# Decoding the gated product's weights in pairs of tiles

## The chip, the cores and the metric

The kernel runs on one core of one Trainium2 chip. The metric is the device time of one execution in microseconds (us), the median of several runs. PE is the matmul engine, PEld its weight loads, DVE the vector engine, ACT the scalar engine, POOL the third elementwise engine, and SP the engine whose queue issues all the transfers.

## What is computed

Three stages follow one another. The first is a gated linear recurrence over 768 steps for 4 batches of 8 heads (head size 48); its output is one row of 384 for each of 3072 tokens. The second is a gated product with 1536 hidden columns, the third a product through `h - tanh(h)` with 2048 hidden columns.

```python
# 1: per head, decay a = a_re + i a_im with its size limited to 0.999
new_re = ar * S_re - ai * S_im
new_im = ar * S_im + ai * S_re
S_re, S_im = new_re + k v^T, new_im
y[t] = q[t] @ S_re
# 2:
gate = 1 / (1 + exp(-(x @ w_gate)))
x = (gate * (x @ w_val)) @ w_out
# 3:
h = x @ w_in
out = (h - tanh(h)) @ w_out2
```

## The kernel before

The recurrence is worked in 24 chunks of 128 steps (names with c), two chunks to a block (names with j, 12 blocks of 256 tokens). For each chunk ACT and DVE make angles and magnitudes out of the tile `ri` (lines 454 to 516 on ACT, 461 to 562 on DVE), scale and turn q and k (tiles `qk`, `qs`, `ks`, lines 566 to 578 on POOL and DVE), and PE makes scores, outputs and a new state (lines 617 to 682). Line 600 or 602 copies a chunk's output into `x`, the input of the gated product.

The weights of the gated product are 36 tiles of 128x384 in DRAM: for each of 12 slices f of hidden columns, tiles 0 and 1 (gate and value, both used in line 884 or 888) and tile 2 (the way back, line 930 or 935). They arrive as 64-bit words, two int32 to a weight, and are decoded on the chip by class `Decoder`, one tile to a `tick`: a transfer into a place for raw words (line 286), two ACT instructions in `word_sign` (lines 64 and 66), two DVE instructions in `word_value` (lines 72 and 75). There are six places of 384 words (`ring1`); the transfer of tile s waits until tile s-6 has been through line 75. The decoded tiles (`whole`) serve block 0; behind their last use there, `part` splits each into a high part (ACT, line 314) and a low part (DVE or POOL, line 317), tile `whl`, which all the later blocks use. The six places then hold `whl` of slices 4 to 6.

`moe1` walks block by block and slice by slice. Block 0 goes in two halves (A: chunk 0, Z: chunk 1), 24 short steps, and its last six steps alternate with the first six of block 1. Between those steps stand the instructions of the recurrence for later chunks, and `dec1.ready` calls as many ticks as the next slice needs. The first 12 ticks stand ahead of that, spread evenly over the preparation of chunks 0 and 1. On PE, DVE, ACT and POOL a scheduler then settles the order of instructions, with its own timeline; on SP the order is that of the code, so a transfer that waits holds every later one.

From the second block on nothing is decoded for the gated product. The weights of the third stage have a decoder of their own (`dec2`), whose first DVE instruction starts at 359.1 us.

Of the kernel before, what the change touches and what calls it, by code (L numbers as in the profile page):

```python
# [8 lines left out]
F32 = mybir.dt.float32  # L9
F32R = mybir.dt.float32r  # L10
BF16 = mybir.dt.bfloat16
I32 = mybir.dt.int32
U8 = mybir.dt.uint8
AF = mybir.ActivationFunctionType
ALU = mybir.AluOpType
# [6 lines left out]
NF1, NF2 = FF1 // 128, FF2 // 128  # L22
# [22 lines left out]
F_SLOPE = RS[7] * 1e-6 * 0.5566  # L45

POOLED = ((9, 10), (3, 4, 9, 10), (3, 4, 6, 10), (2, 3, 4, 6, 9, 10, 11), (3, 4, 5), (10,))
TICKS, TICK_FROM, TICK_TO, BEFORE = 12, 0.0, 1.0, 0
LEAD, LEAD_BLOCKS = 0.6, 2.5
SKEW = 6  # L50
EARLY = 6
# [5 lines left out]
def word_sign(nc, raw, sg, direct=False):  # L57

    hi = raw[:, :, 1].bitcast(F32)
    if not direct:
        nc.scalar.activation(sg, hi, AF.Sign)
    nc.scalar.activation(hi, hi, AF.Copy, scale=2.0 ** -112)  # L64
    top = raw.rearrange("p c two -> p (c two)").bitcast(U8).rearrange("p (c eight) -> p c eight", eight=8)[:, :, 3]
    nc.scalar.activation(raw[:, :, 0], top, AF.Identity, scale=1.0 / 32.0, bias=-31.0 / 64.0)  # L66


def word_value(nc, raw, sg, w, direct=False):
    if direct:  # L70
        wi = w.bitcast(I32)
        nc.vector.scalar_tensor_tensor(
            wi, raw[:, :, 1], 3, raw[:, :, 0], ALU.logical_shift_left, ALU.bitwise_or
        )
        nc.vector.scalar_tensor_tensor(  # L75
            wi, raw[:, :, 1], -2 ** 31, wi, ALU.bitwise_and, ALU.bitwise_or
        )
    else:
        nc.vector.scalar_tensor_tensor(
            raw[:, :, 0], raw[:, :, 1], 3, raw[:, :, 0], ALU.logical_shift_left, ALU.bitwise_or  # L80
        )
        nc.gpsimd.tensor_tensor(w, raw[:, :, 0].bitcast(F32), sg, ALU.mult)
# [161 lines left out]
def kernel(ctx: ExitStack, tc: tile.TileContext, ri, qk, vv, w1, w2, out):  # L244
    nc = tc.nc
    w1i = w1.bitcast(I32)
# [5 lines left out]
    wp = fast.enter_context(tc.tile_pool(name="wp", bufs=1))  # L252
# [21 lines left out]
    class Decoder:  # L274
        def __init__(self, src, nf, nparts, ring, depth, low, spill=None):
            self.src, self.nparts, self.n, self.ring, self.depth, self.low = src, nparts, nf * nparts, ring, depth, low
            self.spill = spill
            self.W, self.F, self.raw, self.sg = {}, {}, {}, {}
            self.loaded = self.tick_no = 0

        def load(self, upto):
            while self.loaded < min(upto, self.n):
                s = self.loaded
                self.raw[s], self.sg[s] = self.ring(s)
                src = self.src[s // self.nparts, s % self.nparts]
                nc.sync.dma_start(out=self.raw[s], in_=src.rearrange("p (c two) -> p c two", two=2))
                self.loaded += 1

        def tick(self):
            k = self.tick_no  # L290
            self.tick_no += 1
            if self.spill is not None and 0 <= k - 2 < self.n:
                self.split(k - 2)
            if 0 <= k - 1 < self.n:
                self.value(k - 1)
            self.load(k + 1)
            if k < self.n:
                word_sign(nc, self.raw[k], None, True)
            while self.loaded < self.n and self.loaded - self.depth(self.loaded) <= k - 2 and self.loaded <= k + 4:
                self.load(self.loaded + 1)  # L300

        def value(self, s):
            if self.spill is not None:
                word_value(nc, self.raw[s], None, self.sg[s], True)
                return
            f, p = s // self.nparts, s % self.nparts
            self.F[f, p] = whole_tile(f, p)
            word_value(nc, self.raw[s], None, self.F[f, p], True)

        def part(self, f, p, after):  # L310

            w = self.F.pop((f, p))
            hl = wp.tile([128, 2, 384], F32R, tag=f"w{SLOT[f, p]}", name="whl")
            ins = nc.scalar.copy(hl[:, 0], w)
            tc.add_manual_dep(ins.ins, after.ins.name, mybir.DependencyInfo(
                mybir.DependencyClass.NoSync, mybir.DependencyReason.DATA), reason="weights whole until then")
            self.low[(f * self.nparts + p) % len(self.low)].tensor_tensor(hl[:, 1], w, hl[:, 0].bitcast(F32), ALU.subtract)
            self.W[f, p] = hl

        def split(self, s):  # L320
            w = self.sg.pop(s)
            hl = self.raw[s].rearrange("p c two -> p (c two)").rearrange("p (two c) -> p two c", two=2).bitcast(F32R)
            nc.scalar.copy(hl[:, 0], w)  # L323
            eng = self.low[s % len(self.low)]
            eng.tensor_tensor(hl[:, 1], w, hl[:, 0].bitcast(F32), ALU.subtract)  # L325
            self.W[s // self.nparts, s % self.nparts] = hl
            nc.sync.dma_start(out=self.spill[s], in_=hl.bitcast(F32))

        def ready(self, s):
            while self.tick_no < min(s, self.n) + 1:  # L330
                self.tick()

    def ring0(s):
        return (stg.tile([128, 384, 2], I32, tag="raw", name="raw"),
                stg.tile([128, 384], F32, tag="sg", name="sg"))


    SLOT = {}
# [6 lines left out]
    halves = {}  # L345

    def whole_tile(f, p):
        if (f, p) == (NF1 - 1, 2):
            return stg.tile([128, 384], F32, tag="last", name="wlast", bufs=1)
        k, half = (24 + f, p) if p < 2 else (18 + f // 2, f % 2)  # L350
        if half == 0:
            halves[k] = wp.tile([128, 2, 384], F32, tag=f"w{k}", name="whole2")
        return halves[k][:, half]

    def ring1(s):
        return wp.tile([128, 384, 2], I32, tag=f"w{12 + s % 6}", name="raw"), None

    dec1 = Decoder(w1i, NF1, 3, ring1, lambda s: 6, (nc.vector, nc.gpsimd))


    mask = ap1.tile([128, 128], BF16, name="mask")
# [499 lines left out]
    A, Z, ALL = slice(0, CH), slice(CH, N1), slice(0, N1)  # L861
# [7 lines left out]
    until = [0.0]  # L869
# [74 lines left out]
    def moe1(units, extra):  # L944
        done = [0]

        def run_to(at):
            while done[0] < len(units) and units[done[0]][0] < at:
                units[done[0]][1]()
                done[0] += 1  # L950

        last = len(order) - NF1
        for n, (j, f, cols) in enumerate(order):
            if n == last:
                run_to(until[n])
                open2()
            dec1.ready(min(3 * f + 4, 36) if j == 0 and cols is A else 36 if j > 1 else 0)
            gv(n)
            if n >= 1:
                split(n - 1)  # L960
            run_to((until[n] + until[n + 1]) / 2)
            extra(2 * (n - last) + 1)
            if n >= LAG1:
                outp(n - LAG1)
                jo, fo, co = order[n - LAG1]
                if jo == 0 and co is Z:
                    dec1.part(fo, 2, gated[n - 1])
            if n == last - (NB - 3) * NF1 + LAG1:
                early.close()
                gvp[2] = ph1.enter_context(tc.tile_pool(name="pgv2", bufs=1, space=PSUM))  # L970
            gate(n)
            if j == 0 and cols is Z:
                dec1.part(f, 0, gated[n])
                dec1.part(f, 1, gated[n])
            run_to(until[n + 1])
            extra(2 * (n - last) + 2)
# [10 lines left out]
    with tc.manual_schedule(engines={mybir.EngineType.SP}):  # L987
# [1 line left out]
        load_ri(1)  # L989
        load_qk(0)  # L990
        load_v(0)
        dec1.load(2)
        load_qk(1)
        load_v(1)
        setup()
# [21 lines left out]
        def open2():  # L1017
            flag_sum()
            att.close()
            P2["x0"] = ph2.enter_context(tc.tile_pool(name="m2x", bufs=1, side="right"))  # L1020
            P2["xr"] = ph2.enter_context(tc.tile_pool(name="m2r", bufs=2, side="right"))
            P2["h"] = ph2.enter_context(tc.tile_pool(name="p2h", bufs=3, space=PSUM, side="right"))
            P2["t"] = ph2.enter_context(tc.tile_pool(name="m2t", bufs=2, side="right"))
            P2["g"] = ph2.enter_context(tc.tile_pool(name="m2g", bufs=3, side="right"))
# [4 lines left out]
        def load_w2(upto):  # L1029
            while len(W2) < min(upto, 2 * NF2):  # L1030
                s = len(W2)
                hl = wp.tile([128, 2, 384], F32R, tag=f"w{SLOT[s // 3, s % 3]}", name="whl")
                nc.sync.dma_start(out=hl.bitcast(F32), in_=w2d[s])
                W2[s // 2, s % 2] = hl

# [89 lines left out]
        for n in range(LAG2, total + LAG2):  # L1125
            i, f = divmod(n, NF2)
# [79 lines left out]
```

## Time and profile before

| | us |
|---|---|
| median of 3 runs | 1128.53 (1127.44 to 1130.26) |
| the profiled execution, its own time | 1129.34 |
| its span, first to last instruction | 1127.6 |
| PE busy | 1050.3 |
| DVE busy | 885.4 |
| ACT busy | 829.3 |
| POOL busy | 158.4 |

The span is what the views show; the 1.7 us between it and the execution's own time lie outside of the instructions. The profiled execution is 0.8 us above the median. Over the whole span PE is busy for 93%, but that share is an average over a start, in which PE waits for DVE and ACT, and a long stretch in which it hardly waits at all.

### The profile page before, as it was taken

Reading aid. Unit: us, or ns where it says so; the run is one execution under the profiler, and the core shown is the slowest. Engines: PE = TensorE matmul, PEld = TensorE weight load, DVE = VectorE, ACT = ScalarE, POOL = GpSimd, SP = SyncE. Lnnn points to the kernel's source line nnn. Section 1 sums busy time; section 2 is a strip of 40 time slices with the busy share of each in tenths; the row PEclk is TensorE's granted clock in tenths of the full one; section 3 lists DMA queues with packets and bytes.
Section 4 is the critical chain, followed back from the end, with each engine's and each line's share of the span. In section 5 each row is a group of like instructions: output and inputs, shape, how many; then the busy total and the mean of one; then the engine's idle time right before and its main releaser. Section 6 shows DMA issues by size and latency. Waiting matters only on the chain.

```text
span 1127.6 us, 22170 instructions
## 1 busy us (share of the span) xinstructions
PE 1050.3 (93%) x8782; PEld 982.3 (87%) x8782; DVE 885.4 (79%) x1475; ACT 829.3 (74%) x1828; POOL 158.4 (14%) x126
## 2 busy tenths in 40 slices
PE   0597999999999999998999999999999999999996
PEld 0486899899999999997998989999998989999996
DVE  6899885987778798989998743587878788787875
ACT  8698785887878897977988573566767676676764
POOL 2335431011001212122213200000000000000000
PEclk9998999999999999999999999999999999999999
DMA  6356003122112344453344446700101010010000
GB/s 228 129 196 190 29 18 88 36 71 74 46 59 60 129 141 133 136 181 104 124 157 123 154 150 246 259 1 1 56 1 56 1 56 2 1 57 1 28 1 31
DMA packets 36400, 100.21 MB, mean 89 GB/s; under 512 B 4128, under 2 KB 7200, under 8 KB 36288
## 3 DMA queue, kind: packets, MB, share of 16 engines
q1 hardware_dynamic: 36288, 98.71, 26.7%
q8 instruction: 71, 1.16, 0.4%
q14 instruction: 41, 0.34, 0.1%
HBM read 76.68 MB, written 22.02 MB: 88 GB/s over the span
## 4 chain that ended last, share of the span: by engine, by line
PE 64%; DVE 13%; ACT 13%; DMA 6%; issue 3%; POOL 1%; SPq 0%; DVEq 0%; ACTq 0%; POOLq 0%
PE h L1070 18%; PE o L1096 17%; PE gv L888 14%; PE acc L935 7%; DMA ri<-in_ri_dram 3%; DMA raw<-in_w_dram 2%; PE gv L884 2%; PE xps L751 2%; PE sc L716 1%; ACT raw L64 1%; DVE suf L549 1%; ACT raw L66 1%; PE gps L781 1%; DVE gh L912 1%; DVE sg L75 1%
## 5 line engine op out<-in xcount | busy, mean ns | idle before, releaser
L888 PE MATMUL gv<-x,whl 128*128 128x256 f32 x2376 | 314.6, 286 | 3.2 <-ACT x L602 2.6
L888 PEld LDWEIGHTS gv<-x,whl 128*128 128x128 f32 x2376 | 295.4, 192 | 8.4 <-issue 3.4
L1096 PE MATMUL o<-whl,gh 128*128 128x384 f32 x1152 | 216.6, 337 | 0.6 <-ACT gh L1082 0.6
L1070 PE MATMUL h<-x2h,whl 128*128 128x512 f32 x864 | 216.0, 394 | 0.0
L1096 PEld LDWEIGHTS o<-whl,gh 128*128 128x128 f32 x1152 | 203.6, 188 | 9.3 <-ACT gh L1082 0.9
L1070 PEld LDWEIGHTS h<-x2h,whl 128*128 128x128 f32 x864 | 160.9, 188 | 29.9
L935 PE MATMUL acc<-gh,whl 128*128 128x256 f32 x1188 | 174.3, 290 | 2.5 <-DVE gh L912 2.2
L935 PEld LDWEIGHTS acc<-gh,whl 128*128 128x128 f32 x1188 | 153.1, 192 | 7.2 <-DVE gh L912 3.1
L89 ACT ACTIVATE s<-h 128x512 f32<-128x512 f32 x96 | 57.8, 602 | 114.5 <-PE h L1070 114.4
L1083 DVE TENSOR_TENSOR gh<-g,gh 128x512 fp32r<-128x512 f32 x96 | 66.3, 690 | 43.8 <-ACT gh L1082 43.5
L912 DVE TENSOR_TENSOR gh<-g,gh 128x256 fp32r<-128x256 f32 x132 | 73.9, 561 | 30.3 <-ACT gh L911 29.2
L97 DVE TENSOR_TENSOR th<-h,th 128x512 f32<-128x512 f32 x96 | 66.4, 691 | 31.6 <-ACT th L95 30.7
L896 ACT ACTIVATE th<-gv 128x256 f32<-128x256 f32 (+1 forms) x156 | 56.3, 361 | 38.8 <-PE gv L888 30.4
L903 DVE SCALAR_TENSOR_TENSOR g<-th,gv 128x256 f32<-128x256 f32 x132 | 54.3, 413 | 37.8 <-ACT th L896 36.7
L98 DVE COPY_PREDICATED g<-mk,th 128x512 f32<-128x512 int32 x96 | 72.3, 754 | 1.0
L911 ACT CAST gh<-g 128x256 fp32r<-128x256 f32 x132 | 52.8, 401 | 26.2 <-DVE g L903 25.7
L91 DVE SCALAR_TENSOR_TENSOR g<-g,s 128x512 f32<-128x512 f32 x96 | 65.5, 682 | 3.3 <-ACT g L90 3.3
L1082 ACT CAST gh<-g 128x512 fp32r<-128x512 f32 x96 | 59.2, 617 | 11.3 <-DVE g L98 11.0
L92 DVE TENSOR_TENSOR g<-g,h 128x512 f32<-128x512 f32 x96 | 65.0, 678 | 3.1
L566 POOL TENSOR_TENSOR qk<-qk,suf 112x512 f32<-112x512 f32 x21 | 31.2, 1484 | 253.3 <-DMA qk<-in_qk_dram 102.4
L325 POOL TENSOR_TENSOR raw<-sg,raw 128x384 fp32r<-128x384 f32 x32 | 40.6, 1269 | 166.7 <-ACT raw L323 129.1
L96 ACT ACTIVATE mk<-s 128x512 f32<-128x512 f32 x96 | 60.8, 633 | 0.0
(165 smaller groups left out, 1697.5 us busy)
## 6 DMA issues: line engine op xcount, KB each, us to landing
raw<-in_w_dram SPq DMA_DIRECT2D x68, 384.0 KB, 5.1
ri<-in_ri_dram SPq DMA_DIRECT2D x30, 448.0 KB, 5.3
w2d<-raw SPq DMA_DIRECT2D x32, 384.0 KB, 4.1
whl<-w2d SPq DMA_DIRECT2D x32, 384.0 KB, 5.0
qk<-in_qk_dram SPq DMA_DIRECT2D x24, 448.0 KB, 4.9
v<-in_vv_dram SPq DMA_DIRECT2D x24, 320.0 KB, 3.5
x2d<-x SPq DMA_DIRECT2D x12, 384.0 KB, 2.3
x2r<-x2d SPq DMA_DIRECT2D x12, 384.0 KB, 3.7
```

The lines of the kernel that those rows point to most:

```text
L91: nc.vector.scalar_tensor_tensor(g, g, TC * TB, s, ALU.add, ALU.mult)
L92: nc.vector.tensor_tensor(g, g, ps, ALU.mult)
L96: nc.scalar.activation(mk, s, AF.Relu, bias=-0.0625)
L97: nc.vector.tensor_tensor(th, ps, th, ALU.subtract)
L98: nc.vector.copy_predicated(g, mk.bitcast(I32), th)
L888: nc.tensor.matmul(ps[:, part], w[:, wi, cs], x[:, xi, kt], start=(k == 0), stop=(k == 8))
L912: nc.vector.tensor_tensor(gh[:, 1], g, gh[:, 0].bitcast(F32), ALU.subtract)
L935: nc.tensor.matmul(o, w[:, wi, cs], gh[:, gi], start=(f == 0 and k == 0 and (m == 0 or m == 2 and not half)), stop=(f == NF1 - 1 and k == ...
L1070: nc.tensor.matmul(ps.rearrange("p (z c) -> p z c", z=2), w[:, wi, cs], x[:, xi, :, kt], start=(k == 0), stop=(k == 8))
L1082: nc.scalar.copy(gh[:, 0], g)
L1083: nc.vector.tensor_tensor(gh[:, 1], g, gh[:, 0].bitcast(F32), ALU.subtract)
L1096: nc.tensor.matmul(a[t], gh[:, gi, cs], w[:, wi], start=(f == 0 and k == 0), stop=(f == NF2 - 1 and k == 2), skip_group_check=True)
```

## The change

The class `Twos` takes the place of `Decoder` for the gated product. A step takes two tiles: gate and value of one slice, or tile 2 of two neighbouring slices, in the order g0, o0, g1, g2, o1, g3, and so on, 18 steps (P0 to P17 below). Its transfer, its two ACT instructions and its two DVE instructions each cover both tiles, 768 columns. Only the last step of the kind o has its DVE work in two halves. There are three places for two tiles each (`d0` to `d2`) instead of six for one, in the same amount of memory; the transfer of step s waits until step s-3 has been through line 75, and is issued at most two steps ahead of the ACT work. Six ticks instead of 12 stand in the preparation. The three places hold `whl` of slices 4 to 6 afterwards, as the six did.

```diff
-TICKS, TICK_FROM, TICK_TO, BEFORE = 12, 0.0, 1.0, 0
+TICKS, TICK_FROM, TICK_TO, BEFORE = 6, 0.0, 1.0, 0
...
+    class Twos:
+
+        def __init__(self):
+            self.seq = []
+            for f in range(NF1):
+                self.seq += [("g", f)] + ([("o", f // 2)] if f % 2 == 0 else [])
...
+        def load(self, upto):
+            while self.loaded < min(upto, self.n):
+                s = self.loaded
+                kind, k = self.seq[s]
+                self.raw[s] = wp.tile([128, 2, 384, 2], I32, tag=f"d{s % 3}", name="raw")
+                src = w1i[k, 0:2] if kind == "g" else w1i[2 * k:2 * k + 2, 2]
+                nc.sync.dma_start(out=self.raw[s], in_=src.rearrange("q p (c two) -> p q c two", two=2))
+                self.loaded += 1
+
+        def value(self, s):
+            kind, k = self.seq[s]
+            raw = self.raw.pop(s)
+            if (kind, k) == ("o", NF1 // 2 - 1):
+                for q in range(2):
+                    self.F[2 * k + q, 2] = whole_tile(2 * k + q, 2)
+                    word_value(nc, raw[:, q], None, self.F[2 * k + q, 2], True)
+                return
+            both = wp.tile([128, 2, 384], F32, tag=f"w{24 + k if kind == 'g' else 18 + k}", name="whole2")
+            word_value(nc, raw.rearrange("p q c two -> p (q c) two"), None, both.rearrange("p q c -> p (q c)"), True)
...
+        def tick(self):
+            k = self.tick_no
+            self.tick_no += 1
+            if 0 <= k - 1 < self.n:
+                self.value(k - 1)
+            self.load(k + 1)
+            if k < self.n:
+                word_sign(nc, self.raw[k].rearrange("p q c two -> p (q c) two"), None, True)
+            while self.loaded < self.n and self.loaded - 3 <= k - 2 and self.loaded <= k + 2:
+                self.load(self.loaded + 1)
...
+        def place(self, f, p, dtype):
+            if 4 <= f < 7 and p < 2:
+                if p == 0:
+                    self.six[f] = wp.tile([128, 2, 2, 384], dtype, tag=f"d{f - 4}", name="whl")
+                return self.six[f][:, p]
+            return wp.tile([128, 2, 384], dtype, tag=f"w{SLOT[f, p]}", name="whl")
...
-    def ring1(s):
-        return wp.tile([128, 384, 2], I32, tag=f"w{12 + s % 6}", name="raw"), None
-
-    dec1 = Decoder(w1i, NF1, 3, ring1, lambda s: 6, (nc.vector, nc.gpsimd))
+    dec1 = Twos()
...
-            dec1.ready(min(3 * f + 4, 36) if j == 0 and cols is A else 36 if j > 1 else 0)
+            dec1.ready(dec1.at['g', f] + 2 if j == 0 and cols is A else dec1.n if j > 1 else 0)
...
-        dec1.load(2)
+        dec1.load(1)
...
-                hl = wp.tile([128, 2, 384], F32R, tag=f"w{SLOT[s // 3, s % 3]}", name="whl")
+                hl = dec1.place(s // 3, s % 3, F32R)
```

Lines after 288 move: line 286 is 332 in the changed kernel, and a line between 361 and 956 is 42 higher (line 454 is 496, line 633 is 675).

The scheduler answers with another order in the first part of the program; the last 1490 instructions on DVE and the last 6745 on PE stand as before. Three places follow. The first is on ACT, behind the second table load for the sines (line 510, 552 in the changed kernel), where chunk 1's angles and magnitudes stand beside chunk 0's first transposed keys (`kt`). Before:

```order
L510 ACT_TABLE_LOAD
L633 COPY kt_317<-ktp_318 128x448
L533 ACTIVATE A_266<-ri_127 112x512
L534 ACTIVATE B_267<-ri_127 112x512
L455 ACTIVATE thC_302<-ri_264 112x512
L456 ACTIVATE thB_301<-ri_264 112x512
L538 ACTIVATE C_268<-A_266 112x512
L495 ACTIVATE D_236<-ri_127 112x512
L64 ACTIVATE raw_275<-raw_275 128x384
L66 ACTIVATE raw_275<-raw_275 128x384
```

Of the change, the same place:

```order
L552 ACT_TABLE_LOAD
L575 ACTIVATE A_241<-ri_127 112x512
L576 ACTIVATE B_242<-ri_127 112x512
L580 ACTIVATE C_243<-A_241 112x512
L581 ACTIVATE A_241<-A_241 112x512
L582 ACTIVATE C_243<-C_243 112x512
L537 ACTIVATE D_217<-ri_127 112x512
L538 ACTIVATE D_217<-D_217 112x512
L675 COPY kt_286<-ktp_287 128x448
L497 ACTIVATE thC_278<-ri_239 112x512
```

Seven instructions on chunk 1, which stood behind the copy of `kt`, now stand ahead of it, and no decoding stands near it.

The second place is on DVE, at the same time: the scan over chunk 1's angles (`ri<-keep,ri`). Before:

```order
L75 SCALAR_TENSOR_TENSOR whole_384<-raw,whole_384 128x384
L490 SCALAR_TENSOR_TENSOR ri<-keep,ri 112x512
L72 SCALAR_TENSOR_TENSOR whole_384<-raw 128x384
L75 SCALAR_TENSOR_TENSOR whole_384<-raw,whole_384 128x384
L622 TENSOR_TENSOR pt<-sc_278,mask 128x512
L544 SCALAR_TENSOR_TENSOR B<-A,B 112x512
```

Of the change:

```order
L620 TENSOR_TENSOR qs<-qk,ri 112x4x128
L532 SCALAR_TENSOR_TENSOR ri<-keep,ri 112x512
L586 SCALAR_TENSOR_TENSOR B<-A,B 112x512
L587 SCALAR_TENSOR_TENSOR A<-C,B 112x512
L591 SCALAR_TENSOR_TENSOR suf<-A,sufs 112x511
L542 SCALAR_TENSOR_TENSOR ri<-D,ri 112x512
```

Behind the scan there stood a tile to decode; now chunk 1's magnitudes follow at once.

The third place is on ACT, further on, where the steps P10 to P14 are decoded (raw_632, raw_639, raw_693, raw_739, raw_746, in this order; `th` is a gate of block 0, `whl` the high part of a split tile). Of the change:

```order
L64 ACTIVATE raw_639<-raw_639 128x768
L66 ACTIVATE raw_639<-raw_639 128x768
L938 ACTIVATE th_705<-gv_695 128x128
L938 ACTIVATE th_724<-gv_711 128x128
L374 CAST whl_728<-whole2_269 128x384
L374 CAST whl_731<-whole2_269 128x384
L374 CAST whl_759<-whole2_224 128x384
L64 ACTIVATE raw_693<-raw_693 128x768
L66 ACTIVATE raw_693<-raw_693 128x768
L64 ACTIVATE raw_739<-raw_739 128x768
L66 ACTIVATE raw_739<-raw_739 128x768
L64 ACTIVATE raw_746<-raw_746 128x768
```

Five steps stand there with two gates and three splits between them; before, no more than three tiles in a row were decoded without another instruction of ACT.

## Rows read from the trace of the kernel before

**Rows 1.** Busy microseconds of each engine in stretches; PEclk is the granted clock share.

```profile
20.00:30.00 10.00, 0.00 (x0) 0.00 (x0) 9.79 (x17) 9.95 (x18) 5.29 (x2) 1.00 0.19 58
30.00:40.00 10.00, 6.04 (x52) 5.15 (x52) 5.72 (x11) 5.47 (x12) 0.91 (x1) 1.00 0.66 223
40.00:50.00 10.00, 7.20 (x67) 6.15 (x68) 10.00 (x20) 9.76 (x21) 3.67 (x2) 1.00 0.30 103
110.00:120.00 10.00, 10.00 (x77) 9.24 (x79) 8.42 (x21) 7.65 (x18) 2.34 (x2) 0.69 0.01 3
130.00:140.00 10.00, 8.11 (x73) 7.80 (x72) 8.81 (x14) 9.08 (x20) 7.91 (x6) 1.00 0.22 73
150.00:160.00 10.00, 10.00 (x90) 9.28 (x89) 6.92 (x12) 7.36 (x20) 1.60 (x2) 1.00 0.01 2
250.00:300.00 50.00, 50.00 (x548) 47.91 (x546) 38.37 (x70) 40.14 (x99) 5.69 (x4) 1.00 0.16 51
```

**Rows 2.** The tile raw up to 140 us: instructions (ns min/median/max), waits, landings.

```profile
L64 ACT ACTIVATE raw<-raw x36: 523/557/590, 12.1 to 107.9; 128x384 f32<-128x384 f32 x36
L75 DVE SCALAR_TENSOR_TENSOR whole<-raw,whole x35: 525/550/2158, 13.7 to 114.6; 128x384 int32<-128x384 int32 x35
  ACT raw L66: 7.1, 5
  DMA raw<-in_w_dram: 0.4, 1
DMA to landing us min/median/max: 2.8/5.6/9.4
```

**Rows 3.** Timeline of ACT: start us, us, then the instruction, wait in brackets.

```profile
11.62 0.61 ACT L455 ACTIVATE thC<-ri 112x512 f32<-112x512 f32 x1
12.13 0.52 ACT L64 ACTIVATE raw<-raw 128x384 f32<-128x384 f32 x1
12.56 0.52 ACT L66 ACTIVATE raw<-raw 128x384 int32<-128x384 uint8 x1
...
28.75 1.28 ACT L510 ACT_TABLE_LOAD   x1
33.46 0.53 ACT L633 COPY kt<-ktp 128x448 f32<-128x448 f32 x1 [3.43 <-PE ktp L632]
```

**Rows 4.** Timeline of DVE, early stretch, same columns.

```profile
13.12 0.56 DVE L72 SCALAR_TENSOR_TENSOR whole<-raw 128x384 int32<-128x384 int32 x1 [3.06 <-ACT raw L66]
13.71 0.56 DVE L75 SCALAR_TENSOR_TENSOR whole<-raw,whole 128x384 int32<-128x384 int32 x1
...
32.16 1.02 DVE L72 SCALAR_TENSOR_TENSOR whole<-raw 128x384 int32<-128x384 int32 x2
33.10 0.69 DVE L472 TENSOR_TENSOR ri<-thA,thC 112x512 f32<-112x512 f32 x1
...
34.71 1.22 DVE L490 TENSOR_TENSOR_SCAN ri<-keep,ri 112x512 f32<-112x512 uint8 x1
39.22 0.56 DVE L72 SCALAR_TENSOR_TENSOR whole<-raw 128x384 int32<-128x384 int32 x1 [3.30 <-ACT raw L66]
```

**Rows 5.** SP's queue: a wait in total, then timeline rows of SP, one of ACT.

```profile
SPq L286 <- DVE whole L75: 31.2, 11, 5.8
...
72.23 17.16 SPq L286 DMA_DIRECT2D raw<-in_w_dram  x9
...
90.70 0.43 SPq L412 DMA_DIRECT2D ri<-in_ri_dram  x1
...
97.69 0.63 ACT L454 ACTIVATE thA<-ri 112x512 f32<-112x512 f32 x1 [2.75 <-DMA ri<-in_ri_dram]
```

**Rows 6.** Timeline of PE and DVE around the first products of block 1.

```profile
57.11 2.93 PE L884 MATMUL gv<-x,whole 128*128 128x128 f32 x12 [5.20 <-DVE gh L900]
...
129.35 0.53 DVE L603 TENSOR_TENSOR x<-xps,x 128x384 fp32r<-128x384 f32 x1
...
131.89 2.40 PE L888 MATMUL gv<-x,whl 128*128 128x256 f32 x18
```

More of the change, by code (lines that the diff above doesn't have):

```diff
@@ L291, in tick @@
             self.tick_no += 1
-            if self.spill is not None and 0 <= k - 2 < self.n:
+            if 0 <= k - 2 < self.n:
                 self.split(k - 2)
@@ L302, in value @@
         def value(self, s):
[L303 to L318, printed above, removed]
+            word_value(nc, self.raw[s], None, self.sg[s], True)
         def split(self, s):
@@ L327, in split @@
             nc.sync.dma_start(out=self.spill[s], in_=hl.bitcast(F32))
+    class Twos:
[3 more added lines that the diff above has]
+                self.seq += [("g", f)] + ([("o", f // 2)] if f % 2 == 0 else [])
+            self.n = len(self.seq)
+            self.at = {u: i for i, u in enumerate(self.seq)}
+            self.W, self.F, self.raw, self.six = {}, {}, {}, {}
+            self.low = (nc.vector, nc.gpsimd)
+            self.loaded = self.tick_no = 0
+        def load(self, upto):
[16 more added lines that the diff above has]
+            word_value(nc, raw.rearrange("p q c two -> p (q c) two"), None, both.rearrange("p q c -> p (q c)"), True)
+            for q in range(2):
+                self.F[(k, q) if kind == "g" else (2 * k + q, 2)] = both[:, q]
+        def tick(self):
[8 more added lines that the diff above has]
+                self.load(self.loaded + 1)
         def ready(self, s):
@@ L331, in ready, with part @@
                 self.tick()
+        def place(self, f, p, dtype):
[4 more added lines that the diff above has]
+            return wp.tile([128, 2, 384], dtype, tag=f"w{SLOT[f, p]}", name="whl")
+        def part(self, f, p, after):
+            w = self.F.pop((f, p))
+            hl = self.place(f, p, F32R)
+            ins = nc.scalar.copy(hl[:, 0], w)
+            tc.add_manual_dep(ins.ins, after.ins.name, mybir.DependencyInfo(
+                mybir.DependencyClass.NoSync, mybir.DependencyReason.DATA), reason="weights whole until then")
+            self.low[(3 * f + p) % 2].tensor_tensor(hl[:, 1], w, hl[:, 0].bitcast(F32), ALU.subtract)
+            self.W[f, p] = hl
     def ring0(s):
@@ L349, in whole_tile @@
             return stg.tile([128, 384], F32, tag="last", name="wlast", bufs=1)
[L350 to L353, printed above, removed]
-    def ring1(s):
-        return wp.tile([128, 384, 2], I32, tag=f"w{12 + s % 6}", name="raw"), None
-    dec1 = Decoder(w1i, NF1, 3, ring1, lambda s: 6, (nc.vector, nc.gpsimd))
+        halves[f] = wp.tile([128, 2, 384], F32, tag=f"w{18 + f // 2}", name="whole2")
+        return halves[f][:, 0]
+    dec1 = Twos()
     mask = ap1.tile([128, 128], BF16, name="mask")
```

## The prediction

> **What bounds the kernel now.** I read the stretches first, since the average over the span hides two regimes. From 150 us on PE is busy without a gap, while DVE and ACT have slack (6.92 and 7.36 of 10 us, later 38.37 and 40.14 of 50) [rows 1]. All decoding for the gated product lies before that: 35 of its 36 tiles start between 12.1 us and 114.6 [rows 2]. In that first part PE starves: 0 of 10 us busy from 20 to 30, 6.04 and 7.20 in the next two stretches, while DVE has 9.79 and later 10.00 of 10, and ACT 9.95 and 9.76 [rows 1]. PE's longest gap behind its start, 5.20 us, ends with a gate on DVE [rows 6]. So the time is a fixed PE stretch behind a start that DVE, and up to 30 us ACT, paces. A microsecond saved on DVE there can be one in the end; one saved at 500 us would be none.
>
> Two rows bound how long that holds. From 110 to 120 us PE is already busy for all 10 us, at 0.69 of its clock, and from 130 to 140 for 8.11 [rows 1]. The first full-precision product of block 1 starts at 131.89, 2.5 us behind the low part of its last input (129.35) on DVE [rows 6].
>
> **The change, part by part.**
>
> *DVE, fewer instructions.* Before, 36 tiles take two each, 72 in all. After, 17 steps take two and the split one four: 38. So 34 starts are removed, and the columns stay. Two independent ones of line 72 take 1.02 us together, one alone 0.56, so the second adds 0.46 [rows 4]. What columns cost I take from line 472: 0.69 us for 512 against 0.56 for line 72's 384 [rows 4], so 128 columns are worth some 0.13 and 384 some 0.39. What a start costs beside columns is 0.46 - 0.39 = 0.07 to 0.08: 34 x 0.08 = 2.7 us. Where line 75 follows its own line 72 directly, the starts lie 13.71 - 13.12 = 0.59 apart, so merging two there saves 0.59 - 0.39 = 0.20: with 17 such pairs and 17 of the other kind, 4.8 us. I take 2.7, since most of the rows are interleaved, and keep 4.8 for the range. It lies on the path, since DVE is full from 40 us.
>
> [...]
>
> *ACT, fewer instructions.* 72 become 36. A start every 0.51 us for 512 columns and 0.43 for 384 [rows 3] leaves 0.08 for 128 columns, so 768 take 0.43 + 3 x 0.08 = 0.67, and 36 mergers save 36 x 0.19 = 6.8 us of ACT. That counts only where DVE waits for ACT. Those waits on decoded words sum to 7.1 us in five cases [rows 2]; 3.06 of them is the first, at 13.12, which hides behind the start of the angles and stays. 3.30 is that of the next paragraph. I put the rest (0.7) at nothing, and the ACT saving itself at nothing: DVE covers it. If DVE were no longer full, up to 6.8 would show.
>
> *The order at 30 to 39 us.* ACT stands idle for 3.43 us ahead of the copy of `kt` (33.46) [rows 3]. Behind the copy stand chunk 1's magnitudes and one tile to decode; DVE, through with its scan at 34.71 + 1.22 = 35.93, waits for that tile until 39.22, 3.30 us [rows 4]. In the changed order seven ACT instructions of 512 columns (7 x 0.51 = 3.6 us) stand ahead of the copy and fill ACT's gap, and DVE has chunk 1's magnitudes ready behind the scan. So the 3.30 goes. What is late next is the angle of chunk 2 (lines 461 and 462 on DVE), which needs the transfer of `ri` and six ACT instructions behind the copy; I leave 0.8 for it, some one and a half of them. Gain 2.5, bounds 0 (another wait of that size) and 3.3.
>
> *Transfers.* As many bytes in 18 instead of 36. Before, a transfer takes 5.6 us to its landing (2.8 to 9.4), and ACT waited for one just once, 0.4 us [rows 2]. After, the first half of a pair waits for the second. SP waits 31.2 us in 11 cases for line 75 to free a place, and the nine transfers from 72.23 on hold the queue for 17.16 us, with the loads of the recurrence behind them; `ri` came so late that ACT waited 2.75 [rows 5]. The changed queue has five transfers there instead of nine, the last of which waits for the same decoded tiles (24), so `ri` comes about as before. I charge 0.8, twice the one wait; bounds 0 and 11 (the second rival).
>
> *Splits, whl and the third stage.* Number and shapes of lines 314 and 317 stay; the tiles in the new places are freed by the same products of slices 4 to 6 as before. Nothing.
>
> **Sum.** -2.7 - 2.5 + 0.8 = -4.4 us. The profiled execution took 1129.34 with a span of 1127.6; it would be 1124.9, and the median, 0.8 lower, 1128.53 - 4.4 = 1124.1.
>
> **Rivals.**
>
> *PE swallows it: no change.* From 110 us on PE has 10.00 of 10, so what DVE does sooner behind that is hidden, and ahead of the first line 888 stand the same 165 products of block 0 as before. For it: PE at 0.69 of its clock from 110 to 120. Against it: the 1.9 us gap from 130 to 140, and that a DVE ahead of time closes the gaps before 110 as well. If only the gain up to 57 us is lost again to a later input of block 1 (129.35), some 1 us is left: 1127.5. It decides if line 603 for chunk 3 ends less than 3 us earlier.
>
> *Three places are too few: slower.* In the third place of the order, P13 needs P10's place and P14 needs P11's. From the end of P11's ACT work to the start of P14's, ACT has two gates, three splits and two steps. Two gates are some 0.4, three splits 3 x 0.43 (their width is line 64's), two steps 4 x 0.67: 4.4 us. In that time P11 must go through DVE (2 x (0.46 + 0.39) = 1.7) and P14's words must land (5.6 as before, 11.2 if twice the bytes take twice the time, 8.4 between). That is 7.3 to 12.9, so ACT waits 2.9 to 8.5, with gates and the angles of chunk 4 queued behind it, and PE and DVE wait for those. With the middle, 5.7, for each of the two rounds of three places from P12 on, 11.4 - 5.2 = +6.2: 1134.7. It decides from 8.6 us of ACT's waits for raw words on (5.2 gained plus 3.4). Against it: the scheduler may have put the rows so late that ACT is never early, and DVE's backlog, not ACT, paces this stretch.
>
> [...]
>
> *The scheduler's new order costs more than it gives, or gives more.* Each way I see some microseconds that no row prices; they widen the range.
>
> **Chances.** A measurement here tells 0.3% (3.4 us) from no change. The forecast 0.46 with its own range of 1119 to 1126; PE swallows it 0.31; the places 0.23. So faster 0.46, same 0.31, slower 0.23. The low end is 4.8 for DVE, 3.3 for the gap and 1.4 of ACT's saving: -9.5, 1119. The high end, 1133, cuts the worst of the second rival.
>
> **What would show it.** Right: 38 instructions of lines 72 and 75 near 0.95 us and 36 of lines 64 and 66 near 0.8; no DVE wait of 3 us near 35; ACT's waits for raw words under 2 us; line 603 for chunk 3 and the first line 888 some 3 to 4 us earlier; PE's rows from 170 us on the same, shifted. Wrong: ACT or SP waiting long for places from 70 to 115 us, or PE's gaps before 110 merely moved.

## The result: slower, by 0.6%

The changed kernel took 1134.92 us (median of 8, 1132.22 to 1138.69), the kernel before in the same runs 1128.61 (median of 8): a ratio of 1.0061, 95% interval 1.0044 to 1.0079. The prediction was 1124.1 with a high end of 1133. The profiled execution took 1133.6, with a span of 1131.6 and the same mean clock, 0.986.

First the stretches of the kernel before, which were not shown, then the same and two more of the changed kernel (columns as in [rows 1]):

```profile
20.00:60.00 40.00, 18.05 (x141) 15.91 (x142) 35.51 (x60) 30.12 (x59) 14.01 (x6) 0.93 0.39 128
60.00:100.00 40.00, 35.10 (x464) 31.88 (x463) 38.37 (x67) 36.18 (x80) 18.70 (x11) 0.94 0.59 199
```

```profile
20.00:60.00 40.00, 20.62 (x165) 18.35 (x166) 39.62 (x55) 31.82 (x54) 11.60 (x7) 1.00 0.44 153
60.00:100.00 40.00, 32.29 (x333) 29.56 (x332) 33.20 (x47) 33.30 (x62) 13.71 (x10) 0.88 0.55 180
...
90.00:100.00 10.00, 4.82 (x29) 4.61 (x28) 8.25 (x10) 7.69 (x15) 4.66 (x3) 0.70 0.95 313
...
130.00:140.00 10.00, 8.77 (x86) 8.33 (x87) 8.08 (x11) 9.46 (x22) 7.14 (x5) 1.00 0.40 125
```

From 20 to 60 us the change does what was forecast: DVE is busy for 39.62 of 40 us instead of 35.51, and PE for 2.57 us more. From 60 to 100 all of it goes: DVE idles for 6.80 us instead of 1.63, and PE does 2.81 less. The instructions that answer to [rows 2], the changed kernel's tile `raw` up to 150 us:

```profile
L64 ACT ACTIVATE raw<-raw x18: 859/914/956, 12.7 to 106.8; 128x768 f32<-128x768 f32 x18
L75 DVE SCALAR_TENSOR_TENSOR whole<-raw,whole x18: 941/950/3262, 15.3 to 117.2; 128x768 int32<-128x768 int32 x17, 128x384 int32<-128x384 int32 x1
  ACT raw L66: 11.1, 7
  DMA raw<-in_w_dram: 2.7, 3
  DVE whole L75: 2.3, 1
DMA to landing us min/median/max: 4.1/7.4/12.4
```

Merged instructions have the forecast length (0.95 us on DVE). But ACT now waits 5.0 us in four cases for raw words (2.7 and 2.3) instead of 0.4, and DVE 11.1 for ACT instead of 7.1. One such wait can be followed from end to end. Timeline rows of the changed kernel, of DVE, ACT (two), DVE (two) and PE:

```profile
86.37 1.37 DVE L75 SCALAR_TENSOR_TENSOR whole<-raw,whole 128x768 int32<-128x768 int32 x1
...
93.48 0.90 ACT L64 ACTIVATE raw<-raw 128x768 f32<-128x768 f32 x1 [2.31 <-DVE whole L75]
...
95.03 0.44 ACT L938 ACTIVATE th<-gv 128x128 f32<-128x128 f32 x2
...
95.18 0.96 DVE L72 SCALAR_TENSOR_TENSOR whole<-raw 128x768 int32<-128x768 int32 x1 [1.72 <-ACT raw L66]
96.06 0.48 DVE L942 SCALAR_TENSOR_TENSOR gh<-th,gv 128x128 f32<-128x128 f32 x2
...
96.39 2.93 PE L926 MATMUL gv<-x,whole 128*128 128x128 f32 x12 [5.18 <-DVE gh L942]
```

The transfers of the same tile that were issued from 86 to 89 us:

```profile
L332 SPq DMA_DIRECT2D raw<-in_w_dram x1: 368/368/368, 87.8 to 87.8; - x1
DMA to landing us min/median/max: 5.6/5.6/5.6
```

Line 75 frees a place at 86.37 + 1.37 = 87.74. SP, whose queue stood at that load, issues it at 87.8, it lands 5.6 us later at 93.4, and ACT starts at 93.48. (The row names line 75 as the releaser, since another one ended at the same moment; the landing fits as well, and that instruction waits for the transfer.) Behind the two ACT instructions stand `th`, the gates' first half, on ACT (95.03), and line 72 on DVE (95.18); behind both stand the gates (line 942, which was 900), and PE, which waits for those, has been idle for 5.18 us. Where it stood idle, from 90 to 100, the granted clock was 0.70 of full speed: 1.00 in each microsecond up to 94, 0.53 in the next and 0.50 from 95 on.

The start of block 1, against [rows 6], on DVE and PE:

```profile
134.58 0.54 DVE L645 TENSOR_TENSOR x<-xps,x 128x384 fp32r<-128x384 f32 x1
...
135.55 2.39 PE L930 MATMUL gv<-x,whl 128*128 128x256 f32 x18
```

Line 645 (before: 603) comes 5.2 us later, the first full-precision product 3.7. That is one part of the loss. Another stands in the last microseconds. Instructions of SP's closing line, of before and then of the changed kernel (whole, and in two windows), and the changed kernel's wait there:

```profile
L1143 SPq EVENT_SEMAPHORE  x8: 17/17/17, 1125.7 to 1126.3; - x8
```

```profile
L1185 SPq EVENT_SEMAPHORE  x8: 17/17/17, 1127.8 to 1130.2; - x8
...
L1185 SPq EVENT_SEMAPHORE  x2: 17/17/17, 1127.8 to 1127.9; - x2
L1185 SPq EVENT_SEMAPHORE  x6: 17/17/17, 1129.8 to 1130.2; - x6
```

```profile
SPq L1185 <- SPq L1185: 4.7, 2, 2.8
```

Before, SP goes through its eight closing waits in 0.6 us; after, it takes 2.4, with 1.9 us between the second and the third. In that gap the transfers of that execution show one single packet, and it is of the queue that carries instructions (window 1127.9 to 1129.8; queue, packets, MB, share):

```profile
q14 instruction: 1, 0.01, 1.4%
```

### The profile page after: what moved, and what is told of

Same layout as the page of the kernel before. It is cut to its first block, busy times and chain, and to the rows that moved or that the text cites. A ratio compares the mean times of both kernels' runs of the same rounds, so it can differ in the third digit from the quotient of the medians.

```text
span 1131.6 us, 22057 instructions
## 1 busy us (share of the span) xinstructions
PE 1053.8 (93%) x8782; PEld 983.9 (87%) x8782; DVE 880.8 (78%) x1441; ACT 826.2 (73%) x1792; POOL 155.1 (14%) x126
## 4 chain that ended last, share of the span: by engine, by line
PE 49%; ACT 20%; DVE 17%; DMA 9%; issue 3%; SPq 0%; DVEq 0%; ACTq 0%
PE h L1112 18%; PE o L1138 17%; DMA ri<-in_ri_dram 7%; PE gv L930 7%; PE acc L977 4%; DMA raw<-in_w_dram 2%; DVE suf L591 1%; ACT raw L64 1%; ACT raw L66 1%; DVE B L604 1%; ACT L552 1%; ACT gh L953 1%; DVE gh L954 1%; ACT th L938 1%; ACT thC L497 1%
## 5 line engine op out<-in xcount | busy, mean ns | idle before, releaser
L954 DVE TENSOR_TENSOR gh<-g,gh 128x256 fp32r<-128x256 f32 x132 | 70.0, 531 | 30.5 <-ACT gh L953 29.5
```

Of the source, the lines that this page charges most:

```text
L954: nc.vector.tensor_tensor(gh[:, 1], g, gh[:, 0].bitcast(F32), ALU.subtract)
```

## Experiments

Each was timed beside the kernel before. Between the measurements the median of the kernel before moved from 1127.4 to 1129.2, so kernels are compared by their ratio to it; 0.001 is 1.13 us. Each interval is some 2 us wide to either side, so a difference between two rows of the table is uncertain by some 3 us, and a smaller one is not shown.

| run | median us | ratio | 95% interval |
|---|---|---|---|
| the change | 1134.92 | 1.0061 | 1.0044 to 1.0079 |
| e1: four places | 1132.96 | 1.0041 | 1.0023 to 1.0059 |
| e2: pairs, 384-column instructions | 1136.12 | 1.0076 | 1.0051 to 1.0102 |
| e3: pairs, single transfers | 1134.62 | 1.0057 | 1.0035 to 1.0080 |
| e4: before, sequence of the change | 1130.69 | 1.0019 | 1.0000 to 1.0037 |
| e5: SP longer by 18 | 1132.06 | 1.0028 | 1.0011 to 1.0046 |
| e6: five places | 1129.92 | 0.9995 | 0.9975 to 1.0015 |
| e7: out tiles later | 1130.50 | 1.0016 | 0.9998 to 1.0033 |
| e8: before, 11 steps early | 1132.26 | 1.0029 | 1.0005 to 1.0053 |
| e9: e5, e6 and e7 together | 1129.96 | 1.0017 | 0.9997 to 1.0036 |
| e10: e9, 384-column instructions | 1133.68 | 1.0050 | 1.0031 to 1.0070 |
| e11: e9, single transfers | 1130.40 | 1.0026 | 1.0007 to 1.0044 |
| e12: e9 with six places | 1127.67 | 0.9998 | 0.9979 to 1.0017 |
| e13: e5 and e6 together | 1127.79 | 0.9991 | 0.9969 to 1.0013 |
| e14: before, 13 steps early | 1130.90 | 1.0012 | 0.9993 to 1.0032 |
| e15: e13, 7 steps early | 1130.97 | 1.0018 | 1.0001 to 1.0036 |
| e16: e13 with six places | 1126.82 | 0.9983 | 0.9966 to 1.0001 |
| e17: e16, 384-column instructions | 1135.94 | 1.0074 | 1.0048 to 1.0100 |
| e18: SP longer by 4 | 1132.10 | 1.0036 | 1.0017 to 1.0055 |

**Places, instructions, transfers, sequence, one at a time (e1 to e4).**

```diff
e1
-self.raw[s] = wp.tile([128, 2, 384, 2], I32, tag=f"d{s % 3}", name="raw")
+self.raw[s] = wp.tile([128, 2, 384, 2], I32, tag=f"d{s % 4}", name="raw")
...
-while self.loaded < self.n and self.loaded - 3 <= k - 2 and self.loaded <= k + 2:
+while self.loaded < self.n and self.loaded - 4 <= k - 2 and self.loaded <= k + 3:
...
-if 4 <= f < 7 and p < 2:
+if 3 <= f < 7 and p < 2:
e2 (word_value alike)
-word_sign(nc, self.raw[k].rearrange("p q c two -> p (q c) two"), None, True)
+for q in range(2):
+    word_sign(nc, self.raw[k][:, q], None, True)
e3
-nc.sync.dma_start(out=self.raw[s], in_=src.rearrange("q p (c two) -> p q c two", two=2))
+for q in range(2):
+    src = w1i[k, q] if kind == "g" else w1i[2 * k + q, 2]
+    nc.sync.dma_start(out=self.raw[s][:, q], in_=src.rearrange("p (c two) -> p c two", two=2))
e4 (on the kernel before, in Decoder)
...
+self.seq += [(f, 0), (f, 1)] + ([(f, 2), (f + 1, 2)] if f % 2 == 0 else [])
...
```

> The changed kernel with four places for raw pairs instead of three (the fourth lies where slice 3's split halves go later, so no memory is added); transfers, 768-column instructions and the first products' place in PE's order stay as in the changed kernel. Theory A (three places are too few: the raw words come late from 80 us on): ACT's 2.7 us of waits for raw words and its 2.3 us wait for line 75 go below 1 us together, SP's 30.6 us of waits for line 75 fall by a third or more, and the time comes back by 3 to 5 us, to 1130 to 1132. Theory B (the scheduler's new order ahead of 60 us, chunk 1's scores in front of block 0's first products): the waits on raw words may go, but the time stays at 1133 to 1137. Theory C (the 768-column instructions themselves, stretched and coarse on DVE): 1133 to 1137 too.

> The changed kernel with its transfers and its three places of two tiles each, but every step decodes its two halves in instructions of 384 columns, so the starts of instructions come back (72 and 72 instead of 38 and 36). Chunk 1's scores stand ahead of the first products in PE's order, as in the changed kernel. Theory C (the 768-column instructions cost it): back to 1128 to 1130. Theories A and B: no gain, 1135 to 1139, the changed kernel's 1134.9 plus up to 2.7 us for the DVE starts that the prediction priced.

> The changed kernel, 768-column instructions and three places of two tiles, but each place is filled by two transfers of 384 KB instead of one of 768 KB. The order in which PE's instructions are written out comes back to that of the kernel before: block 0's first three products stand ahead of chunk 1's scores. Theory B (the order, which the pair transfers bring about): first products at 46 to 48 us again, and the time falls to 1124 to 1129. Theory A (three places): ACT still waits for raw words from 80 us on, and the time stays above 1131. Theory C (768-column instructions): it stays at 1133 to 1137.

> The kernel before, with single tiles, six places and 384-column instructions, but its tiles are loaded and decoded in the sequence of the changed kernel (both gate tiles of a slice, then the out tiles of two slices together). PE's written order of the first products is that of the kernel before. If the sequence of tiles alone cost the time: 1133 to 1136. If, as theories A, B and C all have it, something else did: 1127 to 1130.

The fourth place gives 2 us, less than theory A put on it and within the noise; ACT still waits 3.4 us for words. e2 refutes theory C: with 384 columns the kernel is not faster. e3 does not test theory B. It was written to bring the first products back to 46 to 48 us, but on PE they start where the changed kernel has them, behind 16 of chunk 1's scores (ACT's wait for words is 6.8 us). The first products in the changed kernel, in e3 and, from the last group below, in e13 (five places):

```profile
53.03 4.58 PE L926 MATMUL gv<-x,whole 128*128 128x128 f32 x24
```

```profile
53.62 4.90 PE L927 MATMUL gv<-x,whole 128*128 128x128 f32 x24
```

```profile
55.19 5.49 PE L926 MATMUL gv<-x,whole 128*128 128x128 f32 x24
```

e13 speaks against theory B: its first products stand behind the same 16 scores and come later still (46.83 in the kernel before), and it is no slower than the kernel before. e4, in which the sequence of the tiles is changed and no place, transfer or instruction, is 2 us behind the kernel before, at the edge of the noise.

**SP's end (e5, e18) and five places (e6).**

```diff
e5 (e18: 4 in the place of 18)
-nc.sync.dma_start(out=out[r0:r0 + 128, :], in_=ob)
+if 4 * i + t < 18:
+    for h in range(2):
+        nc.sync.dma_start(out=out[r0:r0 + 128, h * 192:(h + 1) * 192], in_=ob[:, h * 192:(h + 1) * 192])
+else:
+    nc.sync.dma_start(out=out[r0:r0 + 128, :], in_=ob)
e6 (as e1 with five)
-if 4 <= f < 7 and p < 2:
+if 2 <= f < 7 and p < 2:
```

> The changed kernel, with 18 of its first 20 output tiles stored in two halves each, all 40 us or more ahead of the end: SP's program is as many instructions long again as that of the kernel before. Nothing else is changed. In the traces so far SP's eight closing semaphore waits lie within 0.6 us in the three kernels with 36 transfers of raw words, and have a gap of 1.95 us between two of them in the three with 18, at the third or the sixth wait, when every transfer has landed. Theory T (the end of SP's program pays 1.9 us for where its code lies): the gap goes and the time falls by 1.5 to 2.2 us, to about 1133. Against it (the gap is a transfer's late signal, or goes with the pair transfers): the eight waits still take 2.4 us and the time stays at 1134 to 1136.

> The changed kernel with four output tiles stored in halves instead of 18, so SP's program is four instructions longer than the changed kernel's and 14 shorter than that of the kernel before. In the changed kernel the gap of 1.95 us lies between the second and the third of SP's closing waits. If it belongs to a place in SP's code, four more instructions move the waits past it: the eight waits lie within 0.6 us, and the time falls to 1132 to 1133.5, unless the gap then falls on the branch ahead of them and the first wait ends 1.9 us later. If it belongs to the number of transfers of raw words (18 against 36): the gap stays at the third wait and the time at 1134 to 1136.

> The changed kernel with five places for raw pairs (the two more lie where the split halves of slices 2 and 3 go later). Theory A (places, so late raw words that ACT waits for): ACT's waits for raw words, 5.0 us with three places and 3.4 with four, fall below 2, and the time falls below the 1133.0 of four places by another 1 to 2 us, to 1131 to 1132, which is 1129 to 1130 but for the 1.9 us at SP's end. If places are not what costs: 1133 to 1136 as with three or four.

Four instructions more on SP are enough. The closing waits of e18, and the wait in them:

```profile
L1189 SPq EVENT_SEMAPHORE  x8: 17/17/17, 1131.2 to 1131.8; - x8
```

```profile
SPq L1189 <- SPq L1189: 3.4, 1, 3.4
```

The gap is gone although the 18 transfers of raw words are still 18, so it goes with the length of SP's program. That it is the place of SP's closing code, as theory T has it, fits but is not shown directly. The two kernels (e5, e18) gain 2.9 and 2.8 us by their medians (3.7 and 2.8 by the ratios); by the rows 1.9 of that is the gap.

Five places bring 5 us by the medians (7.5 by the ratios), and the gap at SP's end is still in that kernel. That is more than was expected. The wait of SP's loads for line 75 up to 150 us (sum, cases, longest), in the changed kernel, in e6 and then in e16 (six places, below):

```profile
SPq L332 <- DVE whole L75: 30.6, 8, 9.6
```

```profile
SPq L332 <- DVE whole L75: 11.7, 2, 7.1
```

```profile
SPq L332 <- DVE whole L75: 6.6, 1, 6.6
```

**What the sequence and the written order are worth (e7, e8, e14, e15).**

```diff
e7
-self.seq += [("g", f)] + ([("o", f // 2)] if f % 2 == 0 else [])
+self.seq += [("g", f)] + ([("o", f // 2)] if f % 2 == 1 else [])
e8 and e14 (on the kernel before; e14: 13), e15 (on e13, from 6 to 7)
-TICKS, TICK_FROM, TICK_TO, BEFORE = 12, 0.0, 1.0, 0
+TICKS, TICK_FROM, TICK_TO, BEFORE = 11, 0.0, 1.0, 0
```

> The changed kernel with its pairs in another sequence: the out tiles of slices f and f+1 are loaded and decoded behind both slices' gate tiles instead of between them. Theory S (the sequence puts the gate tiles of every odd slice a pair later than they are wanted; the kernel before lost 2.4 us by that sequence alone): 1.5 to 3 us back, 1132 to 1133.5. If the 2.4 us were chance: 1134 to 1136.

> The kernel before with 11 instead of 12 of its decoding steps written out among the setup and the rest behind it: the same work, places, transfers and instructions in a slightly different written order (chunk 1's scores behind the fourth of the first products instead of the third). A control for theory R, that any new order moves the time by as much as this change did: then it would be off by 3 us or more either way, below 1125.5 or above 1131.5. If the order alone is worth less: 1126 to 1131.

> The kernel before with 13 instead of 12 decoding steps among the setup; a second control of what a new written order costs. If the kernel before owes some 2 to 3 us to its own written order (11 steps took 3 us more, the other sequence of tiles 2.4): 1130 to 1133 again. If orders scatter to both sides: 1125 to 1129.

> The kernel with five places and the long SP program, with seven of its steps among the setup instead of six: the same work in a third written order (all of chunk 1's scores behind two first products). If written orders alone scatter by some 3 us: 1124 to 1131, off by 1.5 us or more from the same kernel with six. If the order hardly matters once places suffice: within 1.5 us of it.

e7 gains 4.4 us with three places, more than theory S allowed. But with five places the same edit brings nothing (e13 to e9: 0.9991 to 1.0017), so the sequence has no price of its own: it deals a new order. Read the other way, the same rows limit what can be said of places: in the sequence of e7, five places and the longer SP program bring nothing either (e7 to e9: 1.0016 to 1.0017), though ACT's wait for words falls from 3.6 to 1.0 us, and the first full-precision product of block 1 starts at 131.29 with three places and 131.58 with five. The controls show how much the written order, in which the code hands its instructions to the scheduler, moves alone. The kernel before with one decoding step more or less among the setup is 1.4 and 3.3 us slower by the ratios, and e15 is 3 us off from e13. Each is the same work with the same places. Of these only the 3.3 of e8 is clear of noise; at 1132.26 it is past the 1131.5 that was set as the sign for theory R, so written order remains a rival for some 3 us of any difference here.

**The mends together, and the merged instructions' own price (e9 to e13, e16, e17).**

These are sums of the edits above: e9 is e5, e6 and e7; e10 is e9 and e2; e11 is e6, e7 and e3; e12 is e9 with six places; e13 is e5 and e6; e16 is e13 with six places; e17 is e16 and e2.

> The three mends together: the changed kernel with five places, the out tiles behind both slices' gate tiles, and 18 output tiles stored in halves so that SP's program is as long as before. If the causes add (five places 5.0 us, the sequence 2 to 4.4, SP's end 1.9 to 2.9, against 1134.9): 1123 to 1126, which would be the 4.4 us below the kernel before that the prediction counted for fewer starts and the order at 30 to 39 us. If places and sequence mend the same waits: 1127 to 1129, no faster than the kernel before, and the predicted gain was not there.

> The kernel with the three mends, but decoding in instructions of 384 columns instead of 768, so it prices the merged instructions alone where places are not short. The prediction's terms (2.7 us for 34 fewer DVE starts, ACT's 6.8 at nothing): 2 to 5 us slower than the kernel with the three mends. If the merging is worth nothing once PE paces the end of this part: within 1.5 us of it.

> The changed kernel with five places and the out tiles behind both slices' gate tiles, each place filled by two transfers of 384 KB (36 transfers, so SP's program needs no longer end). If transfers of 768 KB cost in themselves (7.4 us to the landing against 5.6): 1 to 3 us faster than the kernel with the three mends. If it is the places alone: within 1.5 us of it, in either direction.

> The kernel with the three mends and a sixth place, which lies where the split halves of slice 1 go later. Theory A has nothing left to gain, since with five places ACT waits 0.3 us for raw words: within 2 us of the kernel with five. If splits of slice 1 now wait for the last pairs, or the written order (15 of chunk 1's scores ahead of the third product) costs: 2 to 4 us slower than with five.

> The changed kernel with five places and the long SP program, its pairs in the changed kernel's own sequence. If the 1.9 us at SP's end add to the five places (0.9995 of the kernel before with the gap still there): 1126 to 1128, the first kernel of this study below the kernel before. If five places without the pad was a lucky median and the truth lies by the kernel with the three mends (1.0017): 1129 to 1131.

> The changed kernel with six places and the long SP program, pairs in the changed kernel's own sequence. With six places and the other sequence it took 0.9998 of the kernel before. Places beyond five have no wait left to remove, so within 2 us of the kernel with five and the long program; what is over is the written order.

> The kernel with six places and the long SP program, decoding in instructions of 384 columns instead of 768: a second price of the merged instructions where places are not short (the first was 3.7 us, with five places and the other sequence, and 1.2 where three places were short). If the merging is worth 2 us or more also here: 1129 to 1132 against 1126.8. If the 3.7 was the written order: within 1.5 us of it.

The three mends don't add (e9 lies above both forecasts); without the other sequence they come out below the kernel before (e13, e16), though within the interval. e12 is 2.3 us ahead of e9, just past what was expected of a sixth place and within the noise. e11 against e9: with enough places, no price of a 768-KB transfer over two of 384 shows. The kernels with merged instructions are faster in all three pairs, by 1.7 us (e2 to the change, within the noise), 3.7 (e10 to e9) and 10.3 (e17 to e16, more than either forecast) by the ratios. The last two are no price of starts. In e10 and e17 the first products come at 46 us, 8 us sooner than in e9 and e16, and PE then waits for a gate. In e17 the first gates stand behind chunk 2's angles on DVE. Rows of DVE and PE of e17, then of PE of e10:

```profile
54.89 1.75 DVE L622 TENSOR_TENSOR ks<-qk,cosb 112x512 f32<-112x512 f32 x1
56.56 1.75 DVE L516 TENSOR_TENSOR ri<-thA,thC 112x512 f32<-112x512 f32 x1
58.23 0.28 DVE L944 SCALAR_TENSOR_TENSOR gh<-th,gv 128x128 f32<-128x128 f32 x1
...
58.56 2.93 PE L928 MATMUL gv<-x,whole 128*128 128x128 f32 x12 [7.30 <-DVE gh L944]
```

```profile
56.45 2.93 PE L928 MATMUL gv<-x,whole 128*128 128x128 f32 x12 [6.22 <-DVE gh L944]
```

The stretch from 60 to 100 us in e5 (three places), e13 (five) and e16 (six), by which the places can be read without the gap at the end:

```profile
60.00:100.00 40.00, 31.41 (x330) 28.70 (x330) 32.17 (x47) 31.01 (x59) 12.76 (x10) 0.90 0.55 177
```

```profile
60.00:100.00 40.00, 34.01 (x356) 31.25 (x354) 34.76 (x52) 34.28 (x65) 14.75 (x9) 0.96 0.53 185
```

```profile
60.00:100.00 40.00, 32.95 (x404) 29.64 (x402) 39.35 (x55) 36.66 (x71) 18.56 (x11) 1.00 0.43 152
```

DVE's idle time there falls from 7.83 to 5.24 to 0.65 us, and the granted clock rises from 0.90 to 0.96 to 1.00 of full speed; what the clock adds to the gain, no run separates. The first full-precision product of block 1 starts at 136.72, 134.20 and 131.00 us, and the ratios go 1.0028, 0.9991, 0.9983. A profile is one execution: e6 and e13, alike but for the output stores, show 0.3 and 3.3 us of ACT waiting for words. So the row of one run is no exact price. What stands, in this sequence, is that five and six places are faster than three; five and six are not told apart.

## Why the prediction was wrong, step by step

**Transfers: the step that failed.** It charged 0.8 us for three places of two tiles. Five and six places instead bring 4.2 to 5.1 us (e5 to e13 and e16), 7.5 without the longer SP program (the change to e6), each uncertain by some 3. That holds in the changed kernel's own sequence; in that of e7 no price of three places shows, so the runs price three places together with this order, and a share of written order in it stays open. The sign of being wrong came: ACT waited for words four times between 80 and 94 us. The mechanism was written down as the second rival, with a chance of 0.23, and its 1134.7 is within 0.3 us of the median, partly by luck: ACT's waits sum to 5.0 us, not to the 8.6 from which I let it decide, and 1.9 us of the time lie at SP's end, which the rival did not have. The point of decision was wrong in kind. I priced ACT's waits alone, while by the chain followed above the loss is taken where the late words delay what stands behind them on DVE, the gates (DVE's idle time from 60 to 100: 5.2 us more; PE's wait of 5.18).

What the paragraph on transfers worked out, that the fifth transfer would wait for the same 24 tiles, looked at the queue behind the loads (`ri` was in fact issued at 88.73 instead of 90.70) and not at the loop itself: decode, free, issue, land, sign. One turn of that loop, from a freed place to the next decoding on DVE, took from 87.74 to 95.18, 7.4 us, in which DVE found only two more pairs to decode. And what was said against the rival, that DVE's backlog paces this stretch, did not hold: DVE idles for 6.80 us from 60 to 100. For the landing of 768 KB the second rival took 8.4 us as its middle, an estimate; the changed kernel shows a median of 7.4 (4.1 to 12.4).

**DVE, fewer instructions.** Right in sign. DVE's busy time fell from 885.4 to 880.8 us, 4.6, near the bound of 4.8 and not the 2.7 I took. What it is worth in time is not shown: 1.7 us in the one pair that keeps the first products in place, within the noise, and not separable from the order in the other two.

**ACT, fewer instructions.** Counted as nothing, and nothing contradicts it. The saving itself was mis-sized: ACT's busy time fell by 3.1 us, not by 6.8.

**The order at 30 to 39 us.** DVE's wait of 3.30 [rows 4] went, as forecast. The bound of another wait of that size came true too. Rows of DVE, POOL and ACT after:

```profile
28.86 1.75 DVE L514 TENSOR_TENSOR ri<-thA,thC 112x512 f32<-112x512 f32 x1
...
28.16 1.89 POOL L609 TENSOR_TENSOR qk<-qk,B 112x512 f32<-112x512 f32 x1 [3.31 <-DVE B L604]
...
30.64 0.63 ACT L575 ACTIVATE A<-ri 112x512 f32<-112x512 f32 x1 [3.06 <-DVE ri L514]
```

The wait on ACT at 33.46 [rows 3] became one of 3.06 at 30.64, for line 514 and not for the angle of chunk 2, where the prediction looked. DVE was fuller all the same, so the gain of that step was there at 60 us, in PE's 2.57 us, and was lost behind it.

**PE swallows it.** Not what happened: the time did change, and the loss is ahead of PE's full stretch. By its letter its sign came, since line 645 is 5.2 us later and so less than 3 us earlier; the sign did not tell this rival from the second.

**The scheduler's new order.** It was given no price, only a wider range. The controls put 1.4 to 3.3 us on it, and each new order of the kernel before (e4, e8, e14) came out slower, e8 alone clear of noise.

**SP's end.** No step had it: 1.9 us.

The account, by the ratios: e16, with both mended, is 1.9 us below the kernel before (3.8 faster to 0.1 slower), where the sum without its 0.8 for transfers stood at 5.2, so a part of the forecast gain did not come at all. About 5 us for the places and 1.9 for SP's end come on top: 6.9 - 1.9 = +5.0, against 6.9 measured (6.3 by the medians). The rest is within the intervals; how much of it, of the price of the places and of the gain that did not come is written order stays open. e16 is the fastest kernel of the study, though its interval touches no change.

## What to carry to other kernels

When a buffer is made twice as large and half as many, work out one turn of its loop (free, issue, land, use) from the profile's rows, and ask who stands behind the late instruction on the next engine, not only how long the first one waits. Where a scheduler deals the order anew, try a neutral edit first: here it moved the time by up to 3 us, more than half of the gain that was forecast. And test a suspected cause in more than one order: the places that paid in one sequence showed no gain in another. Look at the last microseconds of the queue engine too before a small difference is put down to the loop.

## What the runs showed of the hardware

SP's end: in the five kernels whose SP program has the changed kernel's length (the change, e1, e2, e6, e7), SP's closing line shows two waits for itself, the shorter of 1.9 to 2.1 us; in all the others it shows one, of 2.5 to 3.4. The eight closing waits together take 2.4 us in the changed kernel and 2.5 in e1, against 0.6 in the kernel before, e3, e5 and e18. In the changed kernel no packet of data moves in the gap (1127.9 to 1129.8), only one of the instruction queue. With four more instructions on SP the gap is gone (e18).

Line 75 took 0.95 us in the median, but up to 3.26, and that one ran while POOL was at work. Rows of DVE and POOL of the changed kernel:

```profile
97.61 3.26 DVE L75 SCALAR_TENSOR_TENSOR whole<-raw,whole 128x768 int32<-128x768 int32 x1
...
97.22 1.59 POOL L609 TENSOR_TENSOR qk<-qk,B 112x512 f32<-112x512 f32 x1
98.77 1.28 POOL L617 TENSOR_TENSOR ks<-qk,ri 112x512 f32<-112x512 f32 x1
```

POOL's two instructions cover 97.22 to 100.05, and line 75, which reads two tiles, ends 0.8 us behind them, about its own length. Of three others that started within an instruction of POOL, two took 1.23 us (at 62.79) and 1.37 (at 86.37), but the third 0.94 (at 104.49, within line 620 on POOL, 103.98 to 106.57). So the rows show the overlap and not what sets the length, and no run here took that apart.
